# The first unit of scores of each batch's last, short block of tokens gets its earliest place one later

## The chip, the cores and the metric

The kernel runs on one core of a Trainium2 chip. The metric is the device time of one execution in microseconds (us); the median of several runs counts, and lower is better. One profiled execution gives the trace that the views below are read from.

## The reference

The kernel computes attention with the heads mixed twice, and a feed-forward network with a gate behind it:

```
# q, k, v: 8 batches x 12 heads x 448 tokens x 64
scores = (q @ k^T) / 8                        # per batch and head, 448 x 448
scores = einsum('bhij,hg->bgij', scores, w_pre)   # heads mixed, 12 x 12
attn   = softmax(scores) over j
attn   = einsum('bhij,hg->bgij', attn, w_post)    # heads mixed again
x      = (attn @ v), heads side by side       # 3584 tokens x 768
h      = x @ w_in                             # 768 -> 2048
out    = (h - tanh(h)) @ w_out                # 2048 -> 768
```

All of it is in float32; the feed-forward weights are split into parts by a conversion that runs during the attention.

## The kernel before

**Blocks, groups, places.** The 448 tokens of a batch are cut into four blocks of 120, 120, 120 and 88 tokens, so 32 blocks in all, numbered i = 0 to 31; the short one is i = 3, 7, 11, ..., 31. Ten tokens times 12 heads make a group of 120 rows (12 groups in a block, 9 in a short one), 360 groups in all. Two groups make a pair. The attention is a loop over 180 *places* (line 1262): place p takes pair p through the mixing of the heads and the softmax, and between these steps stand the other jobs that a list, `todo[p]`, gives to this place. On TensorE a place is, in this order:

- `premix(p)` (L920): four instructions (eight rows in the trace) that mix the heads of the pair's scores into two `ps_p` banks. The start of these rows is where a place begins in this text.
- the jobs of `todo[p]`
- `mix(p - 1)` (L957): the second mixing and the transposing of the pair before, which needs the factors `wr`.

VectorE then takes the maxima of place p (`mx`, L929) and ScalarE the exponentials (`e`, L931). The next place makes of their sums the reciprocals (`zs`, VectorE, L938 and L939) and of these the factors `wr` (GpSimd, L940), which `mix` waits for.

**The jobs.** All of them use the four banks `ps_m`/`ps_q` in turn.

- `prep_q(i, 0)`, `prep_q(i, 1)` (L842): transposes the queries of block i; ScalarE (`qh`, L855) and VectorE (`ql`, L857) take them out.
- `prep_k(b, hp)` (L816): the same for two heads of keys; `kk`, L827 on ScalarE and L828 on VectorE.
- `scores(i, hp)` (L876): six products for one pair of heads of block i into two banks. ScalarE and VectorE copy one bank each (L881) into the tile `s` of the block. A unit of scores is two of these jobs, three units make a block.
- `values(i, 0)`, `values(i, 1)` (L1000): the products with v, half a block each; VectorE copies the result to `x` (L1018).
- `load_q`, `load_k`, `load_v`: DMAs from the inputs.

**The tile `s` and the gathers.** `s` holds one block's scores for all heads, and there are two such tiles (`bufs=2`, L741), so block i writes where block i - 2 stood. A DMA on SyncE's queue, `gather(t)` (L909, `t<-s`), fetches group t's rows out of `s` into one of eight tiles `t`, three places ahead of its `premix`: place p issues the gathers 2p + 6 and 2p + 7. The copies of `scores(i, 0)` therefore have to wait until the last gather of block i - 2 has landed.

**Queues.** SyncE issues nearly all DMAs of this stage, in program order: the gathers of a place first, then up to six entries of a queue (loads, and the results that leave), and entries of a second queue with the traffic of the conversion of the feed-forward weights (`cr` in, `wi`/`ss`/`wo`/`ts` out, L767). The conversion (`narrow_quad`, L72) advances one phase in every place that is not in the set `short`, with work on VectorE (L81, L82, L90, L91, L94), ScalarE (L86, L99) and GpSimd (L84 to L129).

**The order.** The planner (L1154 to L1240) sets `todo`. Each unit of scores has an earliest and a latest place; for unit x of block i + 1 these are `e` and `hi`, where `f0`, `f1` are the first groups of blocks i and i + 1:

```
lo = max(0, (f0 - 1) // 2 - 2)
hi = f1 // 2 - 4
e = lo + 2 * x if lo + 4 <= hi else lo + (hi - lo) * x // 2
```

`lo` is the place behind the one that issues the last gather of block i - 1, whose tile `s` block i + 1 takes over. Values have such bounds too. The planner goes through the places in order and gives each one unit, the most urgent that may go, alternating between scores and values; afterwards a unit beside an empty place is split into two single `scores`. `prep_q` of a block is put at the place ahead of its first scores, `load_q` of the next block at the place behind that, and `prep_k` at the first place from a due one that is light enough and far enough behind the last use of its buffer. Within these rules every engine runs its instructions in the order written.

Of the kernel before, what the change touches and what calls it, by code (L numbers as in the profile page):

```python
# [148 lines left out]
def kernel_body(  # L149
# [524 lines left out]
    def pair_step(s, q, late, units, between):  # L674

        def product(i, ph, start):
            n = 7 * (s * NQ + q) + i
            more_wa(n + 6)
            name = WA[i][1]
            xs = [(ff.xs[name + "h"][:, c], ff.xs[name + "l"][:, c]) for c in range(HK)]  # L680
            products(ph, ff.wa.pop(n), xs, start, True)

        def rest(i):
            between(i)
            res.units(units[i])

        X, Y = hbank(), hbank()
        product(0, X, True)
        h01 = work("h01")
        nc.scalar.copy(h01[:, 1], X)  # L690
        if late:
            late.v0()
        rest(0)

        product(1, Y, True)
        nc.vector.tensor_add(h01[:, 1], Y, h01[:, 1])
        if late:
            late.v1()
        rest(1)

        product(2, X, False)
        if late:
            late.v2()
        h23 = work("h23")
        nc.scalar.mul(h23[:, 0], X, -1.0)
        if late:
            late.v3()
        rest(2)

        product(3, Y, True)  # L710
        if late:
            late.v4()
        nc.scalar.mul(h01[:, 0], Y, -1.0)
        rest(3)

        product(4, X, False)
        nc.vector.tensor_sub(h01[:, 0], h01[:, 0], X)  # L717
        if late:
            late.v5()
        g1 = Gate(h01, False)  # L720
        g1.a1()
        rest(4)

        product(5, Y, False)
        nc.vector.tensor_sub(h23[:, 0], h23[:, 0], Y)
        g1.a2()
        g1.d1()
        rest(5)

        product(6, X, False)  # L730
        nc.scalar.copy(h23[:, 1], X)
        g1.d2()
        g1.a3()
        rest(6)
        return Late(s, q, g1, Gate(h23))

    with ExitStack() as st:
# [344 lines left out]
        for w in range(2):  # L1082
            for at in AT[w]:
                x = repeat[:, w, at : at + HP].rearrange("p (i h) -> p i h", i=GH)
# [7 lines left out]
        for w in range(2):  # L1092
            for a in range(2):
                if w == 0:
                    x = both[:, w, a].rearrange("p (i g) -> p i g", i=GH)
                    of, step = ps_w[:, w, :].unsqueeze(1).to_broadcast([P, GH, H]), [[H, GH], [0, H]]
                else:
                    x = both[:, w, a].rearrange("p (g i) -> p g i", i=GH)
# [55 lines left out]
        halved = []  # L1154
        for i in range(len(blocks)):

            f0, f1, f2 = first[i : i + 3]
            if i + 1 < len(blocks):
                lo = max(0, (f0 - 1) // 2 - 2)
                hi = f1 // 2 - 4  # L1160
                for x in range(0 if i else 1, 3):
                    e = lo + 2 * x if lo + 4 <= hi else lo + (hi - lo) * x // 2
                    halved.append((e if i else x - 1, hi, "s", i + 1, x))
            for x in range(2):
                halved.append(((f1 - 1) // 2 + 2, f2 // 2 + 1 if f2 < NG else NPL + 7, "v", i, x))
        at_s, at_v, p, kind = {}, {}, 0, None
        window = {i: (lo, hi) for lo, hi, k, i, _ in sorted(halved, reverse=True) if k == "s"}
        while halved:
            ready = sorted((x for x in halved if x[0] <= p), key=lambda x: (x[1], x[3:]))
            if ready:  # L1170
                x = ready[0]
# [3 lines left out]
                if x[2] == kind and other and x[1] > p + 1:  # L1175
                    x = other[0]
                halved.remove(x)
                _, _, kind, i, n = x
# [11 lines left out]
        def held(p):  # L1190
            return [a for f, *a in todo[p] if f is scores]

        for p in range(1, NPL):
            if any(f in (scores, values) for f, *a in todo[p]):
                continue
            for of, n in ((p - 1, 1), (p + 1, 0)):
                if len(held(of)) == 2 and window[held(of)[n][0]][0] <= p <= window[held(of)[n][0]][1]:
                    i, hp = held(of)[n]
# [133 lines left out]
    late, left = None, 4 * NQ  # L1332
    for s in range(NS):
        more = s + 1 < NS
        for p in range(NQ):
# [16 lines left out]
            late = pair_step(s, p, late, share, between)  # L1352
# [16 lines left out]
        late = None  # L1369
# [33 lines left out]
```

## Time and profile before

| | |
|---|---|
| median of 3 runs | 1688.39 us (1685.31 to 1690.2) |
| profiled execution | 1691.88 us, of it 1690.2 us span |
| TensorE busy (PE) | 1654.1 us, 98% of the span |
| VectorE (DVE), ScalarE (ACT), GpSimd (POOL) busy | 1235.9, 1090.9, 613.9 us |
| the 180 places | 25.9 to 834.7 us of the span |

PE is TensorE, DVE is VectorE, ACT is ScalarE, POOL is GpSimd and SP is SyncE, which only issues DMAs. A line such as L957 is a line of the kernel; `ps_o<-wr,e` reads "writes ps_o, reads wr and e". In the view of waits, `A <- B: total, times, longest` says how long A's engine stood idle until B ended; in the timeline this stands in brackets behind a row. In the table by stretches, a row gives the stretch, its length, each engine's busy time, TensorE's granted clock (1.00 is full speed), the mean busy share of the DMA engines and GB/s.

### The profile page before, as it was taken

Reading aid. Unit: us, or ns where it says so; the run is one execution under the profiler, and the core shown is the slowest. Engines: PE = TensorE matmul, PEld = TensorE weight load, DVE = VectorE, ACT = ScalarE, POOL = GpSimd, SP = SyncE. Lnnn points to the kernel's source line nnn. Section 1 sums busy time; section 2 is a strip of 40 time slices with the busy share of each in tenths; the row PEclk is TensorE's granted clock in tenths of the full one; section 3 lists DMA queues with packets and bytes.
Section 4 is the critical chain, followed back from the end, with each engine's and each line's share of the span. In section 5 each row is a group of like instructions: output and inputs, shape, how many; then the busy total and the mean of one; then the engine's idle time right before and its main releaser. Section 6 shows DMA issues by size and latency. Waiting matters only on the chain.

```text
span 1690.2 us, 40990 instructions
## 1 busy us (share of the span) xinstructions
PE 1654.1 (98%) x16068; PEld 1380.8 (82%) x16068; DVE 1235.9 (73%) x1939; ACT 1090.9 (65%) x1896; POOL 613.9 (36%) x824
## 2 busy tenths in 40 slices
PE   8999999999999999999999999999999999999999
PEld 6777777777777777777788888888888888889999
DVE  5777786877867777776497999868778868778422
ACT  4777776677767677776576776556667356666331
POOL 2577666767666677664100111201111101012100
PEclk9999999999999999999999999999999999999999
DMA  9878788798978979875778899989999989988993
GB/s 191 232 249 239 248 245 253 236 269 256 260 229 260 257 246 261 263 238 201 229 248 321 286 324 319 346 288 343 330 324 358 358 272 338 325 321 321 412 413 134
DMA packets 322672, 475.08 MB, mean 281 GB/s; under 512 B 105648, under 2 KB 255664, under 8 KB 322480
## 3 DMA queue, kind: packets, MB, share of 16 engines
q1 hardware_dynamic: 305660, 414.34, 76.7%
q0 software_dynamic: 16512, 57.68, 8.6%
q8 instruction: 128, 2.10, 0.5%
q14 instruction: 64, 0.52, 0.1%
q10 hardware_dynamic: 308, 0.43, 0.1%
HBM read 274.73 MB, written 120.59 MB: 234 GB/s over the span
## 4 chain that ended last, share of the span: by engine, by line
PE 84%; DVE 6%; DMA 4%; ACT 3%; issue 2%; POOL 1%; SPq 0%; DVEq 0%; ACTq 0%; POOLq 0%
PE ps_o L957 14%; PE ps_m L1000 8%; PE ps_p L920 8%; PE ps_h L289 7%; PE ps_h L292 7%; PE ps_h L290 7%; PE y L532 6%; PE ps_q L876 6%; PE y L530 6%; PE y L531 6%; PE ps_m L842 1%; DMA w<-wo 1%; DMA t<-s 1%; PE ps_m L816 1%; DVE mx L929 1%
## 5 line engine op out<-in xcount | busy, mean ns | idle before, releaser
L957 PEld LDWEIGHTS ps_o<-wr,e 60*112 60x112 f32 (+1 forms) x5760 | 304.0, 175 | 32.7 <-POOL wr L940 17.2
L957 PE MATMUL ps_o<-wr,e 60*112 60x60 f32 (+1 forms) x5760 | 313.0, 258 | 7.0 <-POOL wr L940 5.7
L931 ACT ACTIVATE e<-ps_p,mx 128x448 f32<-128x448 f32 x360 | 225.4, 632 | 110.9 <-DVE mx L929 55.8
L929 DVE TENSOR_REDUCE mx<-ps_p 128x1 f32<-128x448 f32 x360 | 206.6, 616 | 78.6 <-PE ps_p L920 78.1
L967 ACT COPY at<-ps_o 112x960 f32<-112x960 f32 x156 | 153.9, 987 | 104.1 <-PE ps_o L957 103.7
L920 PE MATMUL ps_p<-t,wpre 60*64 60x448 f32 (+1 forms) x1440 | 179.1, 565 | 1.6 <-DMA t<-s 1.6
L940 POOL TENSOR_TENSOR wr<-wpost,zs 128x120 f32<-128x120 f32 x180 | 69.9, 388 | 265.6 <-DVE zs L939 204.8
L1000 PEld LDWEIGHTS ps_m<-at,vr 112*64 112x64 f32 x3072 | 151.2, 139 | 18.5 <-issue 12.9
L1000 PE MATMUL ps_m<-at,vr 112*64 112x120 f32 (+1 forms) x3072 | 164.8, 265 | 0.0
L530 PE MATMUL y<-w,gh 128*128 128x384 f32 x440 | 148.4, 337 | 4.1 <-DMA w<-wo 3.0
L531 PE MATMUL y<-w,gh 128*128 128x384 f32 x440 | 147.6, 336 | 0.0
L532 PE MATMUL y<-w,gl 128*128 128x384 f32 x416 | 140.4, 337 | 2.5 <-DVE gl L448 2.5
L881 DVE COPY s<-ps_q 120x448 f32<-120x448 f32 (+1 forms) x192 | 112.3, 615 | 24.6 <-DMA t<-s 12.5
L876 PEld LDWEIGHTS ps_q<-kk,qh 64*120 64x120 f32 (+1 forms) x768 | 58.6, 173 | 85.2 <-issue 44.6
L876 PE MATMUL ps_q<-kk,qh 64*120 64x448 f32 (+1 forms) x768 | 121.6, 393 | 1.2 <-DVE kk L828 0.5
L881 ACT COPY s<-ps_q 120x448 f32<-120x448 f32 (+1 forms) x192 | 94.8, 535 | 19.9 <-DMA t<-s 9.6
L305 ACT ACTIVATE u<-h 128x1024 f32<-128x1024 f32 x56 | 59.6, 1064 | 72.0 <-DVE h L717 68.1
L645 POOL DMA_DIRECT2D gs<-ga x24 | 17.5, 730 | 242.5 <-DVE ga L328 242.5
L530 PEld LDWEIGHTS y<-w,gh 128*128 128x128 f32 x440 | 82.6, 188 | 9.0 <-issue 4.7
L531 PEld LDWEIGHTS y<-w,gh 128*128 128x128 f32 x440 | 82.6, 188 | 3.3
L442 ACT CAST gh<-gl 128x1024 fp32r<-128x1024 f32 x60 | 62.5, 1041 | 28.7 <-DMA gl<-gs 18.0
L532 PEld LDWEIGHTS y<-w,gl 128*128 128x128 f32 x416 | 78.0, 188 | 3.4 <-DVE gl L448 3.4
(372 smaller groups left out, 3955.6 us busy)
## 6 DMA issues: line engine op xcount, KB each, us to landing
t<-s SPq DMA_DIRECT2D x342, 210.0 KB
wa<-ss SPq DMA_DIRECT2D x96, 384.0 KB
gl<-gs SPq DMA_DIRECT2D x62, 512.0 KB
w<-wo SPq DMA_DIRECT2D x41, 768.0 KB
wa<-wi SPq DMA_DIRECT2D x72, 384.0 KB
w<-ts SPq DMA_DIRECT2D x36, 768.0 KB
gs<-gs POOLq DMA_DIRECT2D x24, 768.0 KB, 8.5
cr<-in_moe_w_in_dram SPq DMA_DIRECT2D x48, 256.0 KB
```

The lines of the kernel that those rows point to most:

```text
L289: nc.tensor.matmul(ph, w[:, c, 0], xh, start=start and c == 0, stop=False, skip_group_check=True)
L530: nc.tensor.matmul(y, gh[:, tok], wh, start=first, stop=False, skip_group_check=True)
L531: nc.tensor.matmul(y, gh[:, tok], wl, start=False, stop=False, skip_group_check=True)
L532: nc.tensor.matmul(y, gl[:, tok], wh, start=False, stop=last, skip_group_check=True)
L876: nc.tensor.matmul(ps[:n, :S], qx[a, hp, :], kx[a, hp % 2], start=(x == 0), stop=(x == 2))
L881: eng(sts[i][:n, 2 * hp + j, :], ps[:n, :S])
L920: nc.tensor.matmul(pss[r][halves[j], :], wpre[k, :], ts[j][k, :], start=True, stop=True)
L929: nc.vector.tensor_reduce(out=mx, in_=ps, axis=AX.X, op=ALU.max, negate=True)
L931: nc.scalar.activation(e, ps, AF.Exp, bias=mx, scale=1.0, accum_out=zs[:, 0, r : r + 1])
L957: nc.tensor.matmul(ps[:CP, j, c * GP : (c + 1) * GP].rearrange("p (h i) -> p h i", i=GI)[:, :, r * GH : (r + 1) * GH], e[k, c * CP : (c + ...
L967: nc.scalar.copy(ats[i0][:, :, :, at : at + 2 * GI].rearrange("p c h (j i) -> p j (c h) i", j=2), ps[:CP, :, : NC * GP].rearrange("p j (x ...
L1000: nc.tensor.matmul(pv[j * D : (j + 1) * D, r, :n], vt[:, j, c, :], ats[i][:, c, 2 * hp + j, :n], start=(c == 0), stop=(c == NC - 1),)
```

## The change

The earliest place of unit 0 of the short block's scores is raised by one (`i % 4 == 2` means that block i + 1 is the short one). Nothing else is edited:

```
                 for x in range(0 if i else 1, 3):
                     e = lo + 2 * x if lo + 4 <= hi else lo + (hi - lo) * x // 2
-                    halved.append((e if i else x - 1, hi, "s", i + 1, x))
+                    late = 1 if i % 4 == 2 and x == 0 else 0
+                    halved.append((e + late if i else x - 1, hi, "s", i + 1, x))
```

The planner answers to it in each of the 8 batches, at four places in a row. For batch 2 (counted from 0; block 11 is its short one) these are places 53 to 56; the other batches' begin at places 8, 31, 76, 98, 121, 143 and 166:

| place | before | after |
|---|---|---|
| 53 | prep_q(11, 0 and 1), values(8, 0) | values(8, 0) |
| 54 | scores(11, 0), scores(11, 1), load_q(12) | prep_q(11, 0 and 1), values(8, 1) |
| 55 | prep_k(3, 2 and 3), values(8, 1) | scores(11, 0), scores(11, 1), load_q(12) |
| 56 | scores(11, 2) | prep_k(3, 2 and 3), scores(11, 2) |
| 57 | scores(11, 3) | the same |

The last batch has no prep_k and no load_q there. The set `short` stays the same.

TensorE in batch 2, before, from the rows behind `premix(53)` on (`ident,qr` is prep_q, `at,vr` values, `kk,qh` and `kk,ql` scores, `ident,kr` prep_k):

```order
L842 MATMUL ps_m<-ident,qr 128x88 x6
L1000 MATMUL ps_m<-at,vr 64x120 x24
L957 MATMUL ps_o<-wr,e 112x12x5 x16
L920 MATMUL ps_p<-t,wpre 64x448 x4
L876 MATMUL ps_q<-kk,qh 88x448 x4
L876 MATMUL ps_q<-kk,ql 88x448 x2
L876 MATMUL ps_q<-kk,qh 88x448 x4
L876 MATMUL ps_q<-kk,ql 88x448 x2
L957 MATMUL ps_o<-wr,e 112x12x5 x16
L920 MATMUL ps_p<-t,wpre 64x448 x4
L816 MATMUL ps_m<-ident,kr 128x112 x8
L1000 MATMUL ps_m<-at,vr 64x120 x24
```

The same stretch with the change, from the rows behind `premix(53)` on:

```order
L1000 MATMUL ps_m<-at,vr 64x120 x24
L957 MATMUL ps_o<-wr,e 112x12x5 x16
L920 MATMUL ps_p<-t,wpre 64x448 x4
L842 MATMUL ps_m<-ident,qr 128x88 x6
L1000 MATMUL ps_m<-at,vr 64x120 x24
L957 MATMUL ps_o<-wr,e 112x12x5 x16
L920 MATMUL ps_p<-t,wpre 64x448 x4
L876 MATMUL ps_q<-kk,qh 88x448 x4
L876 MATMUL ps_q<-kk,ql 88x448 x2
L876 MATMUL ps_q<-kk,qh 88x448 x4
L876 MATMUL ps_q<-kk,ql 88x448 x2
L957 MATMUL ps_o<-wr,e 112x12x5 x16
```

The first scores now stand behind both halves of the values, one `premix` and one `mix` later, and prep_k comes at the place behind them, ahead of the next single `scores` (not shown).

SyncE's queue in the same batch, where `t<-s` are the gathers, `cr` and `ss` the conversion's traffic and `qr` is load_q(12) (a piece of the difference):

```order
 L909 DMA t<-s 120x1x448 x4
-L767 DMA qr<-in_q_dram 120x12x64
 L767 DMA ss_81<-ct 512x1x256
 L767 DMA cr<-in_moe_w_in_dram 128x2x256 x2
 L909 DMA t<-s 120x1x448 x2
+L767 DMA qr<-in_q_dram 120x12x64
```

The gathers keep their order; load_q(12) goes behind three conversion DMAs and two more gathers.

## Prediction

> **What bounds the kernel now.** First the page's head, then the table by stretches for the 180 places of the attention.
>
> ```profile
> span 1690.2 us, 40990 instructions
> PE 1654.1 (98%) x16068; PEld 1380.8 (82%) x16068; DVE 1235.9 (73%) x1939; ACT 1090.9 (65%) x1896; POOL 613.9 (36%) x824
> ...
> 26.00:834.67 808.67, 793.82 (x11629) 613.27 (x11629) 596.75 (x1326) 581.66 (x1309) 509.36 (x639) 0.99 0.83 245
> ```
>
> TensorE is busy 98% of the span, in the attention 793.8 of 808.7 us. It is the bound, and the change takes no matmul away. What can be had is idle time of TensorE (14.9 us here) and time at a lower clock, so I next read the view of waits over this stage for what TensorE and the copies of the scores wait for.
>
> ```profile
> DVE s L881 <- DMA t<-s: 12.5, 3, 6.0
> ...
> PE ps_m L816 <- DVE s L881: 7.9, 4, 4.1
> ...
> PE ps_o L957 <- POOL wr L940: 5.7, 7, 1.3
> ```
>
> Four times the transposes of prep_k (L816) wait for VectorE's copies of scores, 7.9 us in all, and three times such a copy is seen waiting for a gather. To find the four, I cut the stage into places by the eight L920 rows that open each. The table by stretches has first the seven places that hold prep_k and values(., 1) of the first block of a batch (10, 33, 55, 78, 100, 123, 145), then three places with one scores job (79, 101, 102).
>
> ```profile
> 66.67:72.82 6.15, 6.15 (x98) 5.08 (x96) 4.74 (x11) 3.62 (x9) 4.46 (x4) 1.00 0.83 221
> 167.63:176.68 9.05, 7.84 (x98) 6.56 (x97) 6.00 (x14) 4.61 (x10) 4.41 (x7) 0.81 0.95 270
> 268.82:281.63 12.81, 8.71 (x98) 7.44 (x96) 5.09 (x11) 4.43 (x10) 3.38 (x7) 0.73 0.93 274
> 377.00:383.16 6.16, 6.16 (x99) 5.09 (x97) 4.72 (x10) 3.30 (x8) 4.03 (x4) 1.00 0.83 278
> 475.59:482.99 7.40, 6.22 (x98) 5.09 (x97) 4.38 (x10) 4.62 (x10) 3.48 (x6) 1.00 0.93 289
> 580.35:589.56 9.21, 7.83 (x99) 6.56 (x97) 5.09 (x11) 4.43 (x10) 3.46 (x6) 0.81 0.91 251
> 681.86:688.01 6.15, 6.15 (x98) 5.08 (x97) 4.66 (x11) 4.05 (x9) 3.99 (x4) 1.00 0.88 298
> ...
> 383.16:386.37 3.21, 3.21 (x48) 2.32 (x47) 1.92 (x5) 2.94 (x7) 0.39 (x1) 1.00 0.91 225
> ...
> 482.99:487.63 4.64, 3.56 (x49) 2.30 (x47) 4.12 (x12) 2.73 (x6) 1.22 (x2) 0.97 0.87 252
> 487.63:492.29 4.66, 4.66 (x49) 2.92 (x47) 2.11 (x5) 2.85 (x6) 3.07 (x3) 0.66 0.42 159
> ```
>
> The same work takes 6.15 us in batches 0, 3 and 6 and 9.05, 12.81, 7.40 and 9.21 us in batches 1, 2, 4 and 5: 2.90 + 6.66 + 1.25 + 3.06 = 13.87 us too much. In batch 4 the two places behind follow with 4.64 and 4.66 instead of 3.21: 2.88 us. Together 16.75 us. The clock column says why this is twice the idle time of the waits: behind the wait TensorE is granted 0.73 to 0.81.
>
> Now the cause, in batch 2: the timelines of TensorE, VectorE and SyncE.
>
> ```profile
> 268.82 0.98 PE L920 MATMUL ps_p<-t,wpre 60*64 60x448 f32 x8
> 273.90 1.76 PE L816 MATMUL ps_m<-ident,kr 112*128 112x112 f32 x8 [4.10 <-DVE s L881]
> 275.59 4.40 PE L1000 MATMUL ps_m<-at,vr 112*64 112x120 f32 x48
> ...
> 266.04 1.16 DVE L929 TENSOR_REDUCE mx<-ps_p 128x1 f32<-128x448 f32 x2 [0.45 <-PE ps_p L920]
> 273.22 1.15 DVE L881 COPY s<-ps_q 88x448 f32<-88x448 f32 x2 [6.03 <-DMA t<-s]
> ...
> 261.31 3.50 SPq L767 DMA_DIRECT2D ss<-ct  x1
> 264.90 2.06 SPq L767 DMA_DIRECT2D cr<-in_moe_w_in_dram  x2
> 267.05 1.69 SPq L909 DMA_DIRECT2D t<-s  x2
> ```
>
> The two gathers issued from 267.05 are 112 and 113, the last of block 9, whose tile `s` block 11 takes over. SyncE comes to them late, behind the conversion's traffic. They land just ahead of 273.22, where the copy starts; VectorE was free at 267.20 (266.04 + 1.16). So the copies are 6.0 us late, L816 finds no free bank, and TensorE idles 4.10 us. In the other three batches the copies are late by half of that:
>
> ```profile
> 169.15 1.15 DVE L881 COPY s<-ps_q 88x448 f32<-88x448 f32 x2 [3.14 <-DMA t<-s]
> ...
> 477.07 1.15 DVE L881 COPY s<-ps_q 88x448 f32<-88x448 f32 x2 [3.10 <-PE ps_p L920]
> ...
> 582.03 1.15 DVE L881 COPY s<-ps_q 88x448 f32<-88x448 f32 x2 [3.30 <-DMA t<-s]
> ```
>
> In 477.07 the view names TensorE, which had long been done; I read it as the same gather.
>
> **The change part by part.** It adds and removes no instruction. In each batch four places are dealt anew; a place costs TensorE what its matmuls cost, and rows of before show each new kind or its nearest neighbour.
>
> ```profile
> 220.52:225.76 5.24, 5.24 (x90) 4.31 (x88) 3.95 (x8) 2.44 (x6) 4.16 (x5) 1.00 0.92 265
> 259.15:264.99 5.84, 5.84 (x96) 4.82 (x94) 4.53 (x11) 3.56 (x9) 5.09 (x7) 1.00 0.95 243
> 264.99:268.82 3.83, 3.83 (x54) 2.79 (x53) 1.73 (x5) 2.32 (x5) 3.08 (x3) 1.00 1.02 274
> 247.54:251.70 4.16, 4.16 (x57) 3.18 (x55) 3.37 (x7) 2.92 (x7) 1.41 (x2) 1.00 0.85 253
> 251.70:255.29 3.59, 3.50 (x48) 2.32 (x47) 3.13 (x8) 3.24 (x8) 2.16 (x3) 1.00 0.92 241
> ...
> 458.27:461.50 3.23, 3.23 (x48) 2.38 (x46) 2.99 (x8) 2.59 (x7) 2.22 (x3) 1.00 1.06 277
> ...
> 664.70:667.94 3.24, 3.24 (x48) 2.40 (x46) 3.00 (x8) 2.58 (x7) 2.21 (x3) 1.00 0.92 240
> ...
> 48.37:53.15 4.78, 3.50 (x48) 2.32 (x46) 4.61 (x12) 3.41 (x8) 2.08 (x3) 1.00 0.88 216
> ```
>
> Row 1 is values alone (place 44), row 2 prep_q with values (53), row 3 a unit of scores (54), row 4 prep_k with one scores job (50). Before, the four places cost 5.84 + 3.83 + 6.15 + 3.21 = 19.03 us without waits; after, 5.24 + 5.84 + 3.83 + 4.16 = 19.07 us. That is +0.04 us a batch, 0.3 us in eight.
>
> *The copies against the gather.* The scores begin 5.24 + 5.84 = 11.08 us behind the start of the first of the four places instead of 5.84, so 5.24 us later, while the gathers keep their place in SyncE's queue. Of the 6.03 us of lateness in batch 2 about 0.8 us is left, of the 3.1 to 3.3 us in the others nothing. What TensorE bears without a stall follows from batch 2: 6.03 us of lateness became 4.10 us of idle, so about 1.9 us is covered by the `mix` and `premix` that stand ahead of L816. 0.8 us lies inside. So the 16.75 us go, the two places behind batch 4's stall included, since their wait for `wr` came out of the copies' delay. Bounds: 0 gained, if the gathers move with the scores, and 16.75.
>
> *prep_q and values(., 1)* change places with prep_q hidden as before, one place ahead of its scores; values need nothing but what values(., 0) already had a place earlier. I take 0; if the 5.84 did not hold, the nearest rows for what the same place can vary by are 5 and 6, 0.36 us apart, in eight batches 2.9 us either way.
>
> *prep_k beside one scores job.* VectorE gets two `kk` subtractions into this place, ahead of the `zs` that the next place's `wr` and `mix` wait for; TensorE would wait at that `mix`. The trace has this pair of places four times. The place behind took 3.59, 3.23 and 3.24 us (rows 5 to 7), and 4.78 us once (row 8, with one more phase of conversion beside it). From row 6, between nothing and 4.78 - 3.23 = 1.55 us a batch. I take the mean of the three that are like the new places (no conversion phase in the place behind), 0.12 us, in seven batches with prep_k 0.8 us.
>
> *load_q of the next block* is issued one place later, behind two more gathers and in batch 2 behind three conversion DMAs:
>
> ```profile
> 274.13 0.76 SPq L767 DMA_DIRECT2D qr<-in_q_dram  x1
> ...
> 279.08 1.65 SPq L909 DMA_DIRECT2D t<-s  x2
> ```
>
> It would go out at about 280.8 instead of 274.1. With the 6.2 us from 267.05 to 273.22 as a time to land that is 287.0. Its reader, place 59, comes at 259.15 + 19.07 + 3.21 + 3.83 = 285.3, plus 0.9 of `premix`. If SyncE does not come earlier by itself, that is 0.8 us late, in this batch alone. But SyncE's issues here wait on the conversion, which the stalled VectorE had held up; I take 0, with 0.8 us kept for the range. ScalarE's and VectorE's copies move with their matmuls; GpSimd gets no instruction moved.
>
> The sum: 16.75 - 0.3 - 0.8 = 15.6 us. The profiled execution took 1691.88 us and would take 1676.3. The median, 1688.39, lies 3.5 us below it, and the same difference gives 1672.8.
>
> **The clock behind a short wait.** A wait that is left over can cost more than itself. In batch 5 TensorE idled 1.38 us (9.21 less 7.83 busy), and a stretch at half clock followed:
>
> ```profile
> 582.95:586.36 3.41, 3.41 (x30) 3.13 (x30) 1.84 (x6) 3.41 (x9) 2.32 (x3) 0.50 0.76 235
> ```
>
> Half of 3.41 us is 1.7 us; with the 1.38 us of idle that is the 3.06 us lost there. Row 8 is the other bound: 1.28 us of idle (4.78 less 3.50) at a clock of 1.00 all through. So a leftover wait of 1 us costs 1.0 to 2.7 us; I take 2.7, the dearer row, because the stalls in question are like batch 5's. The Trainium skill (TensorE: Matmul & The Clock Gate, Part 1: The HAM clock gate) says that the clock is halved after at least one idle window of about 3.4 us. By that rule only batch 2's wait would have lost clock, and two leftover waits of 1 us would make 1674.8 us of the forecast where the row above makes 1678.2. The trace speaks against it: 1.38 us were enough in batch 5. It agrees on the length of the slow stretch, 3.41 us.
>
> **The rivals.**
>
> 1. *A part comes back.* The copies in batch 2 and the `kk` work leave waits of about 1 us in two to four places, at 2.7 us each: 5.4 to 10.8 us of the 15.6 come back, which gives 1678.2 to 1683.6. For it: rows 5 and 8; against it: rows 6 and 7.
> 2. *The transfers are the bound.* In batch 2 the DMA share is 1.02 in the place ahead of the stall; if transfers set the pace, TensorE waits at a `premix` or for `qr` instead, and the time stays 1688.4. Against it: the share over the stage is 0.83, and batches 0, 3 and 6 run these places without a wait at 0.83 to 0.88.
> 3. *Slower: `mix` waits for `wr` behind the new prep_k place in every batch.* At row 8's 1.55 us and a half clock of 1.7 us, seven batches lose 22.8 us: 1688.4 - 16.45 + 22.8 = 1694.7. It decides from 2.4 us a batch on. Against it: three of four such places lost 0.35 us at most.
>
> **How the numbers follow.** The stalls go with little given back: 62%, 1668 to 1677. Rival 1: 17%. Rival 2: 13%. Rival 3: 8%. A measurement of this kernel tells some 0.3% (5.1 us) from no change: faster by more 79%, within 13%, slower 8%. The range has at its low end all 16.75 us from the fastest run shown (1685.3), 1668, less 1 us; at its high end rival 1 whole and a little of rival 2: 1667 to 1685.
>
> **What would show it.** Right: places 33, 55, 100 and 123, now scores alone, at 3.8 us, the places behind at 4.2, no wait of L816 for `s`, and no clock below 1.00 between 100 and 800 us. Wrong: L881 still waits over 2 us for `t<-s`; or L957 waits for `wr` at places 12, 35, 57; or L842 of place 59 waits for `qr`.

## The result, and the profile after

The changed kernel takes 1680.99 us, the median of 16 runs (1679.35 to 1685.35), beside 1689.76 us (16 runs, 1685.31 to 1696.22) for the kernel before on the same chip: 8.8 us less. The ratio is 0.9949, its 95% interval 0.9938 to 0.9961. The forecast was 1672.8 us, so the direction is right and the gain is little more than half of the 15.6 us. The head of the profile after:

```profile
PE 1654.7 (98%) x16068; PEld 1379.2 (82%) x16068; DVE 1243.4 (74%) x1939; ACT 1091.3 (65%) x1896; POOL 612.8 (36%) x824
```

The profiled execution took 1685.35 us, the longest of the 16. Places 0 to 7, which the change leaves alone, took 36.9 us in it and 31.1 us in the profile of before; this is taken up below. The table by stretches has places 33, 35, 55 to 59, 100 and 123 of the profile after, and then the whole attention:

```profile
175.13:178.96 3.83, 3.83 (x55) 2.78 (x53) 3.71 (x10) 3.61 (x8) 2.61 (x4) 1.00 0.92 295
...
183.08:186.63 3.55, 3.47 (x48) 2.25 (x46) 3.08 (x8) 3.18 (x8) 2.15 (x3) 1.00 0.93 201
...
274.55:278.37 3.82, 3.82 (x55) 2.79 (x53) 2.65 (x5) 3.54 (x8) 2.06 (x3) 1.00 0.83 282
278.37:282.61 4.24, 4.24 (x57) 3.02 (x55) 3.42 (x7) 3.37 (x9) 2.10 (x4) 1.00 0.91 309
282.61:286.46 3.85, 3.54 (x49) 2.36 (x47) 3.70 (x8) 3.48 (x9) 2.16 (x3) 1.00 1.05 250
286.46:291.02 4.56, 4.09 (x55) 2.70 (x53) 4.53 (x9) 2.73 (x8) 3.78 (x5) 1.00 0.83 250
291.02:297.02 6.00, 6.00 (x96) 4.92 (x95) 3.74 (x9) 3.86 (x10) 4.25 (x7) 1.00 0.88 307
475.95:479.78 3.83, 3.83 (x54) 2.79 (x52) 3.71 (x10) 3.60 (x8) 2.61 (x4) 1.00 0.92 292
...
576.94:580.77 3.83, 3.83 (x55) 2.79 (x53) 2.78 (x5) 3.54 (x8) 2.15 (x2) 1.00 0.82 297
...
26.16:828.82 802.66, 793.00 (x11629) 610.27 (x11629) 603.46 (x1326) 582.13 (x1309) 509.97 (x639) 0.99 0.82 247
```

The four stalls are gone: places 33, 55, 100 and 123 take 3.82 or 3.83 us at full clock, where 9.05, 12.81, 7.40 and 9.21 us stood. But places 35 and 57, which took 3.21 us before, now take 3.55 and 3.85, and places 58 and 126 (the latter not shown) take 4.56 and 4.55 instead of 3.88 and 3.86. The attention as a whole is 6.0 us shorter (802.66 against 808.67). The view of waits over the attention says what TensorE and the copies wait for now:

```profile
PE ps_o L957 <- POOL wr L940: 7.6, 11, 1.8
...
DVE s L881 <- PE ps_q L876: 6.2, 13, 1.5
```

There is no row any more of L881 waiting for `t<-s` or of L816 waiting for `s`. In their place `mix` waits for `wr` 11 times, 7.6 us in all, where the view of before had 7 times and 5.7 us. Five of the 11 are new, 1.9 us together, at places 57, 58, 125, 126 and 148. The timelines around places 57 and 58 show the first two. VectorE first:

```profile
276.80 1.15 DVE L881 COPY s<-ps_q 88x448 f32<-88x448 f32 x2
...
282.72 1.16 DVE L828 TENSOR_TENSOR kk<-ps_m,kk 128x448 fp32r<-128x448 f32 x2 [0.83 <-ACT kk L827]
283.79 0.16 DVE L938 TENSOR_SCALAR zs<-zs 128x2 f32<-128x2 f32 x1
...
285.65 1.34 DVE L81 TENSOR_SCALAR cm<-cr 128x512 f32<-128x512 f32 x1
286.91 1.53 DVE L82 TENSOR_SCALAR cr<-cr 128x512 int32<-128x512 int32 x1
288.37 0.15 DVE L938 TENSOR_SCALAR zs<-zs 128x2 f32<-128x2 f32 x1
```

Twice `zs` comes behind other work of VectorE. GpSimd, which makes `wr` of it, in the same stretch:

```profile
284.30 0.39 POOL L940 TENSOR_TENSOR wr<-wpost,zs 128x120 f32<-128x120 f32 x1 [3.46 <-DVE zs L939]
...
285.21 1.50 POOL L96 TENSOR_TENSOR cm<-cr,co 128x512 f32<-128x512 f32 x1
286.79 1.37 POOL L97 TENSOR_TENSOR cm<-cm,cr 128x512 f32<-128x512 f32 x1
288.86 0.39 POOL L940 TENSOR_TENSOR wr<-wpost,zs 128x120 f32<-128x120 f32 x1 [0.70 <-PE ps_q L876]
```

And TensorE, which waits for `wr`:

```profile
284.74 1.78 PE L957 MATMUL ps_o<-wr,e 60*112 60x60 f32 x32 [0.31 <-POOL wr L940]
...
289.30 0.90 PE L957 MATMUL ps_o<-wr,e 60*112 60x60 f32 x14 [0.47 <-POOL wr L940]
```

In place 57, VectorE waits 0.83 us for ScalarE's part of `kk` and takes the two subtractions of the place before at 282.72, then `zs` at 283.79, `wr` follows at 284.30 and `mix` at 284.74, 0.31 us late. In place 58, the conversion's next phase (L81, L82, 2.8 us of VectorE) stands ahead of `zs`, and `mix` is 0.47 us late. That phase stood ahead of `zs` in before too, where the two steps took 0.8 us (last section). The first row is the copy of the moved scores: it no longer waits for anything in the view. The view has 0.31 us of wait in place 57, which grew by 0.64. `mix` begins 2.13 us behind the start of the place (284.74 less 282.61), where before it began 1.59 us behind it (286.52 less 284.93, not shown): 0.54 us later. Part of this does not show as idle time, because TensorE's rows overlap where one job follows on the other: before, the last scores row reached to 286.68. `mix` itself takes 1.78 us instead of 1.69. So the busy time of the place grew as well (3.54 us instead of 3.21).

### The profile page after: what moved, and what is told of

Same layout as the page of the kernel before. It is cut to its first block, busy times and chain, and to the rows that moved or that the text cites. A ratio compares the mean times of both kernels' runs of the same rounds, so it can differ in the third digit from the quotient of the medians.

```text
span 1683.6 us, 40980 instructions
## 1 busy us (share of the span) xinstructions
PE 1654.7 (98%) x16068; PEld 1379.2 (82%) x16068; DVE 1243.4 (74%) x1939; ACT 1091.3 (65%) x1896; POOL 612.8 (36%) x824
## 4 chain that ended last, share of the span: by engine, by line
PE 83%; DVE 6%; DMA 4%; ACT 4%; issue 2%; POOL 1%; SPq 0%; DVEq 0%; POOLq 0%; ACTq 0%
PE ps_o L957 14%; PE ps_m L1000 8%; PE ps_p L920 8%; PE ps_h L289 7%; PE ps_h L290 7%; PE ps_h L292 7%; PE y L532 6%; PE y L530 6%; PE y L531 6%; PE ps_q L876 6%; DMA w<-wo 1%; PE ps_m L842 1%; DMA t<-s 1%; ACT e L931 1%; PE y L502 1%
## 5 line engine op out<-in xcount | busy, mean ns | idle before, releaser
L957 PEld LDWEIGHTS ps_o<-wr,e 60*112 60x112 f32 (+1 forms) x5760 | 304.7, 175 | 36.5 <-POOL wr L940 20.8
L957 PE MATMUL ps_o<-wr,e 60*112 60x60 f32 (+1 forms) x5760 | 314.7, 259 | 8.9 <-POOL wr L940 7.6
L1000 PEld LDWEIGHTS ps_m<-at,vr 112*64 112x64 f32 x3072 | 147.6, 137 | 22.0 <-issue 14.1
L1000 PE MATMUL ps_m<-at,vr 112*64 112x120 f32 (+1 forms) x3072 | 161.1, 261 | 0.0
L881 DVE COPY s<-ps_q 120x448 f32<-120x448 f32 (+1 forms) x192 | 112.4, 615 | 8.9 <-PE ps_q L876 8.5
L881 ACT COPY s<-ps_q 120x448 f32<-120x448 f32 (+1 forms) x192 | 95.0, 536 | 7.0 <-PE ps_q L876 6.7
```

Of the source, the lines that this page charges most:

```text
L881: eng(sts[i][:n, 2 * hp + j, :], ps[:n, :S])
L957: nc.tensor.matmul(ps[:CP, j, c * GP : (c + 1) * GP].rearrange("p (h i) -> p h i", i=GI)[:, :, r * GH : (r + 1) * GH], e[k, c * CP : (c + ...
L1000: nc.tensor.matmul(pv[j * D : (j + 1) * D, r, :n], vt[:, j, c, :], ats[i][:, c, 2 * hp + j, :n], start=(c == 0), stop=(c == NC - 1),)
```

## The experiments

The theory (A): the late gathers cost the four stalls; the move takes them away in the four batches that had them; in the others it brings nothing. The first rival (B): the new dealing of jobs is cheaper by itself, with a stall or without.

**The move in the four stalled batches alone.**

```
-late = 1 if i % 4 == 2 and x == 0 else 0
+late = 1 if i in (6, 10, 18, 22) and x == 0 else 0
```

> The later place is given to the scores of batches 1, 2, 4 and 5 alone, the four in which the copies into s waited for a gather. Theory A (what is gained is those waits, 16.75 us of them in the trace of before, less about 5 us that come back at mix): all of the gain of the full change, 8 to 12 us faster than before, and batch 6 as before (its place 148 at 3.9 us, not 4.4). Theory B (the new dealing of values and prep_k is itself cheaper, in every batch): half of the gain, 4 to 5 us.

1681.46 us (6 runs, 1679.01 to 1685.22), ratio to before 0.9943, interval 0.9925 to 0.9962: 7.7 us less than before on the same chip (1689.11 us), a little under the 8 to 12 expected, and within the noise all of the gain. Its table by stretches has place 33 as it is after, and place 148, in batch 6 that was not moved, as it was before:

```profile
169.94:173.75 3.81, 3.81 (x54) 2.79 (x52) 3.68 (x10) 3.58 (x8) 2.60 (x4) 1.00 0.93 305
...
682.41:686.31 3.90, 3.90 (x55) 2.71 (x53) 3.83 (x9) 3.41 (x9) 3.12 (x5) 1.00 0.83 277
```

**The move in the other four batches alone.**

```
-late = 1 if i % 4 == 2 and x == 0 else 0
+late = 1 if i in (2, 14, 26, 30) and x == 0 else 0
```

> The later place is given to the scores of batches 0, 3, 6 and 7 alone, which had no such wait. Theory A: nothing is gained, 0 to 1 us slower than before, and the stalls of batches 1, 2, 4 and 5 stand in the profile as before (places 33, 55, 100, 123 at 9, 13, 7 and 9 us). Theory B: 4 to 5 us faster.

1690.53 us (12 runs, 1687.18 to 1694.62), ratio 1.0003, interval 0.9987 to 1.0019. Nothing is gained, and B falls. One part of the expectation was missed: the stalls of places 33, 55, 100 and 123, untouched here, were not as long as in the profile of before:

```profile
169.27:175.69 6.42, 6.22 (x98) 5.09 (x96) 4.38 (x10) 4.66 (x10) 3.58 (x7) 1.00 0.95 285
269.13:281.37 12.24, 8.52 (x98) 7.25 (x97) 5.09 (x11) 4.43 (x10) 3.37 (x7) 0.72 0.94 283
...
475.26:481.42 6.16, 6.16 (x98) 5.09 (x96) 4.63 (x11) 4.54 (x10) 3.84 (x6) 1.00 0.89 278
577.26:583.96 6.70, 6.23 (x99) 5.09 (x97) 4.35 (x10) 4.43 (x10) 3.46 (x6) 1.00 0.87 249
```

Only batch 2 stalls as before; in place 100 there is no stall to see. So the price of the stalls moves from execution to execution, or with what the other batches do; the repeated profiles below bear on this. The profiled execution, 1687.65 us, is the second fastest of the 12.

**The order before, with the last gathers sent first.** The scores stay, but at the seven places that issue the last gathers of the block whose `s` is taken over, SyncE holds the conversion's traffic back for one place.

```
-def issue(most):
-    for x in (queue, slow):
+def issue(most, of):
+    for x in of:
...
-issue(6)
+issue(6, (queue,) if p in (7, 30, 52, 75, 97, 120, 142) else (queue, slow))
```

> The kernel before, with the conversion's DMAs held back in one place of each of seven batches (7, 30, 52, 75, 97, 120, 142), so that SyncE issues the last gathers of the block whose s is taken over ahead of them; no other engine's order changes. Theory A (the copies are late because SyncE comes to these gathers late): the gather of batch 2 goes out 5 to 6 us earlier, batch 4's about 5, batch 5's 2.4, batch 1's 0.6; the stalls at places 55, 100 and 123 go, that at 33 keeps 2 to 3 us; 10 to 14 us faster than before, without moving the scores. Theory D (the transfers are the bound, whatever their order): the gathers land at the same time or TensorE waits elsewhere, within 4 us of before.

1683.39 us (12 runs, 1678.10 to 1691.21), ratio 0.9958, interval 0.9938 to 0.9978. The cause is shown: nothing but SyncE's order was touched, and 5.7 us of 1689.11 go. Places 33, 34 and 55 in the table by stretches, and VectorE's copy that waited 6.03 us in batch 2:

```profile
167.96:174.43 6.47, 6.23 (x99) 5.09 (x97) 3.99 (x9) 4.12 (x10) 3.07 (x6) 1.00 0.89 295
174.43:179.56 5.13, 3.46 (x48) 2.24 (x47) 4.52 (x12) 3.06 (x8) 1.74 (x3) 1.00 0.99 241
...
268.45:275.00 6.55, 6.23 (x99) 5.09 (x97) 4.36 (x10) 4.44 (x10) 3.40 (x7) 1.00 0.91 294
...
269.08 1.15 DVE L881 COPY s<-ps_q 88x448 f32<-88x448 f32 x2 [2.25 <-PE ps_o L957]
```

The copy waits 2.25 us, and place 55 falls from 12.81 to 6.55 us, place 123 (not shown) from 9.21 to 6.16. The 10 to 14 us expected were not reached. Less than expected was won in batch 1, where place 33 keeps 0.3 us and place 34, at 5.13 instead of 3.21 us, waits for `wr` (1.67 us of idle); that is 2.2 us, and the rest stays open.

**The change without the conversion's phase beside the new prep_k.** It tests what came back: the phase is left out of the seven places that now hold prep_k and one scores job, and all later phases shift.

```
+short |= {11, 34, 56, 79, 101, 124, 146}
 block0 = Block0()
```

> The changed kernel, with no phase of the conversion in the seven places that now hold prep_k and one scores job (11, 34, 56, 79, 101, 124, 146); the conversion runs one place behind for each. Theory A (mix waits at places 57, 58, 125 and 126 because VectorE has the conversion's three operations and two kk subtractions there ahead of zs): L957's waits for wr at 57 and 125 go and those places take 3.2 to 3.3 us, 2 to 4 us faster than the changed kernel. Theory C (the waits come from the banks or from transfers, not from VectorE's load): the waits stay and the time is that of the changed kernel within 1 us.

1679.68 us (7 runs, 1677.95 to 1688.20), ratio 0.9943, interval 0.9922 to 0.9965; it cannot be told from the change itself, so the 2 to 4 us expected beyond it were missed. Places 57 and 58, and places 166 to 179 together:

```profile
275.66:278.88 3.22, 3.22 (x48) 2.25 (x46) 3.02 (x8) 2.59 (x7) 2.16 (x3) 1.00 0.90 177
278.88:283.23 4.35, 4.09 (x55) 2.71 (x53) 4.32 (x9) 2.88 (x8) 3.56 (x5) 1.00 0.63 228
...
757.74:822.18 64.44, 61.81 (x925) 47.60 (x923) 38.92 (x87) 42.27 (x94) 32.40 (x46) 0.97 0.69 236
```

Place 57 is back at 3.22 us, so its wait needs both, the conversion's phase and `kk`, ahead of `zs`; places 35, 102 and 125 (not shown) are back at 3.22 us too. But place 58 keeps 4.35, and the conversion, ending seven places later, reaches the last places: 64.44 us instead of 61.63 in the profile after (of the 2.8 us, 1.5 are half clock in the last place, which other profiles have too). The saving is shifted, not won.

**Both kernels again, unedited.** Two more profiles of before and two of after, to size the 16.75 us.

> The kernel before, unedited, for a second profile. It sizes the 16.75 us that the prediction took for the four stalls from one execution. In that one batches 1, 2, 4 and 5 lost 2.90, 6.66, 4.13 and 3.06 us, and two of the four stalls were followed by 3.41 to 6.83 us at half clock. Theory A: the idle time of the stalls is steady (about 7.9 us of waits of L816), and the half clock behind them comes and goes, so that places 33, 55, 100 to 102 and 123 together lose anywhere from 9 to 17 us; expected here about 11 us, with stretches at half clock in other places than in the first profile. Theory B: the stalls cost the same in each execution, 16 to 17 us, with half clock behind places 33, 55 and 123 again; then some 4 us that the change should have brought went elsewhere. Time 1685 to 1692 us.

> The kernel before, a third profile, for the spread of the same sum. Theory A: places 33, 55, 100 to 102 and 123 lose 9 to 17 us over 6.15 us for the first four and 3.21 us for the places 101 and 102, not the same as in the second profile. Theory B: 16 to 17 us as in the first. The time and the mean granted clock should go together: 0.001 of the clock is 1.7 us.

> The changed kernel, unedited, for a second profile. In the first, places 0 to 7, whose code the change does not touch, took 36.9 us where they took 31.1 in the profile of before. Theory A: that is a chance of the one execution; here 31 to 33 us, and 1680 to 1682 us in all. Theory B: it belongs to the change; here again about 37 us. Either way what came back behind the moved jobs is steady, as it comes from the order and not from the clock: places 35, 57, 102 and 125 at 3.5 to 3.9 us instead of 3.2, places 58 and 126 at 4.5 instead of 3.85, place 148 at 4.4 instead of 3.9, about 4 to 5 us in all.

> The changed kernel, unedited, timed beside the other and beside before on one chip. 1681 us, 0.995 of before; slow windows of 3.41 us begin at whole multiples of 3.41 us from each other, as in the profiles so far; of the waits of TensorE of 1.0 to 1.4 us in places 4 to 166 those that lie within one such window are followed by half clock about two times in three, those that straddle two windows are not.

The profiled executions took 1689.86 and 1699.08 us (before), 1681.03 and 1685.21 us (after). Six more runs of after had a median of 1681.04 us, against 1688.62 us of before (12 runs) on the same chip, ratio 0.9957, interval 0.9944 to 0.9969. The table by stretches, for places 31 to 75 (batches 1 and 2) and 98 to 142 (batches 4 and 5). First the profile of before that the prediction read:

```profile
157.96:367.33 209.37, 203.59 (x2954) 158.22 (x2953) 156.85 (x345) 148.28 (x335) 141.26 (x179) 0.98 0.85 247
465.92:672.19 206.27, 202.35 (x2954) 156.48 (x2952) 155.62 (x344) 148.33 (x335) 138.06 (x166) 0.98 0.86 251
```

The second profile of before:

```profile
159.04:369.62 210.58, 203.78 (x2955) 158.48 (x2953) 156.80 (x345) 148.30 (x335) 141.07 (x179) 0.98 0.84 246
468.17:670.62 202.45, 199.55 (x2954) 154.49 (x2952) 155.25 (x344) 148.42 (x335) 137.54 (x166) 1.00 0.87 255
```

The first profile of after:

```profile
164.05:366.33 202.28, 200.20 (x2954) 154.34 (x2952) 159.90 (x345) 148.61 (x335) 141.57 (x179) 1.00 0.87 258
464.87:665.75 200.88, 199.79 (x2954) 154.41 (x2952) 159.32 (x344) 148.33 (x335) 138.28 (x166) 1.00 0.87 256
```

And the second:

```profile
157.72:359.54 201.82, 200.28 (x2954) 154.34 (x2953) 160.39 (x344) 148.58 (x335) 141.93 (x179) 1.00 0.87 257
458.11:658.99 200.88, 199.78 (x2955) 154.39 (x2953) 159.26 (x344) 148.35 (x335) 138.27 (x166) 1.00 0.87 258
```

The two stretches summed, those of the third profiles with them, split into TensorE's idle time (length less busy) and busy time:

| profile | length | idle | busy | the stalls* |
|---|---|---|---|---|
| before, first | 415.64 | 9.70 | 405.94 | 16.75 |
| before, second | 413.03 | 9.70 | 403.33 | 13.21 |
| before, third | 415.75 | 10.51 | 405.24 | 15.72 |
| after, first | 403.16 | 3.17 | 399.99 | none |
| after, second | 402.70 | 2.64 | 400.06 | none |
| after, third | 402.29 | 2.41 | 399.88 | none |

*Places 33, 55, 100, 123, 101 and 102 over 6.15 us and 3.21 us, the sum that the prediction made. It leaves out what place 124 lost in the second profile (0.75 us) and place 34 in the third (1.34 us).

Both theories about the size were partly right. The idle time is steady, as A said, and it is half clock that comes and goes; but 13.2 to 16.8 us is a narrower band than A's. The four batches gain 12.1 us in the mean, of it 7.2 us of idle and 4.9 us of busy time, which is half clock less what the matmuls of after are spread out. This is more than the medians show: the three profiled executions of before have a mean of 1693.6 us, above all its medians (1688.39 to 1691.77 us). The profile of the move in the other four batches, where these four batches are as in before, has 7.65 us of idle and 7.95 us of stalls, outside the spread of the three; so the price of a stall moves with what the other batches do as well. Places 0 to 7 of the kernel after took 30.9 us in the second profile and 33.8 in the third, so their 36.9 us in the first are not in every execution. Whether they have to do with the change stays open: `mix` of place 4 waits 1.5 to 2.2 us for `wr` in three of the 12 profiles, all three of kernels with the move in batch 0 (six profiles), though none of their instructions ahead of place 8 differ. What came back is the same in all three, within 0.03 us: places 35, 57, 102 and 125 at 3.55, 3.85, 3.55 and 3.84 us.

**Two attempts at a better version.** The move in the four stalled batches, or in all eight, and the phase left out at four places.

```
-late = 1 if i % 4 == 2 and x == 0 else 0
+late = 1 if i in (6, 10, 18, 22) and x == 0 else 0
...
+short |= {34, 56, 101, 124}
 block0 = Block0()
```

> The move in the four batches that stalled, and the conversion's phase left out of places 34, 56, 101 and 124 alone, the new places with prep_k. Theory A (the wait for wr there comes of the conversion beside kk): places 35, 57, 102 and 125 at 3.2 us, 36, 58, 103 and 126 up by at most 0.5 us, places 166 to 180 at 63.1 us, up by 1.5, since the conversion ends four places later; the time 1679 us, 2 us less than the change as it is, in the range of 1677 to 1681. Rival: what the skipped phases save, the shifted phases take back in other places (as places 36, 103 and 165 did where all seven were left out), and the time is 1681, that of the four batches alone.

1683.68 us (12 runs, 1680.61 to 1689.96), ratio 0.9955, interval 0.9938 to 0.9971, on a chip where before took 1691.77 us: the rival, as by the ratio it cannot be told from the move in the four batches alone (0.9943). The profile shows where the saving went. Places 78 and 145 of the table by stretches, in batches 3 and 6 that were not moved:

```profile
368.45:376.52 8.07, 6.23 (x99) 5.09 (x97) 4.33 (x10) 4.66 (x10) 3.55 (x7) 1.00 0.92 265
...
669.01:676.29 7.28, 6.22 (x98) 5.08 (x96) 4.38 (x10) 4.64 (x10) 3.47 (x6) 1.00 0.94 297
```

They stall now (before they took 6.15 or 6.16 us in every profile but one, where place 145 took 6.80): the conversion, shifted, falls ahead of their last gathers, and in place 78 the copy waits 3.76 us for `t<-s`. Which batch stalls is a matter of where the conversion stands. With the move in all eight batches, as the change has it, and the same four phases left out:

> The change in all eight batches, as it is, with the conversion's phase left out of places 34, 56, 101 and 124 alone. Theory A (moving the scores by one place makes a batch proof against where the conversion's traffic falls; the batches that were left as before are at its mercy, as places 78 and 145 with 8.06 and 7.29 us showed where the same four phases were left out): places 78 and 145, now scores alone, at 3.83 us, no wait of L816 for s, places 35, 57, 102 and 125 at 3.22 us; batches 121:143 and 143:166 within 1 us of the changed kernel's 99.9 and 101 to 103; the time 1679 us, 1677 to 1681. Rival: the shifted phases take back what they save in any order; the time is that of the changed kernel on this chip, or above.

1680.03 us (6 runs, 1676.64 to 1683.44), ratio 0.9953, interval 0.9939 to 0.9967, beside 1681.04 us for the change itself on the same chip. Place 78:

```profile
369.13:372.96 3.83, 3.83 (x54) 2.79 (x52) 2.77 (x5) 3.54 (x8) 2.06 (x3) 1.00 0.82 296
```

Place 145 takes 3.83 us too. In none of the three places of the conversion that were run with the move in all batches (the change, and the phase left out of seven places or of four) did a moved batch stall; that is what the move is good for in the batches that did not need it. In the four batches this version takes 399.4 us, 3.4 less than after in the mean, yet its time cannot be told from that of the change. Part of the 3.4 us is paid in batch 3, where places 76 to 97 take 99.9 us instead of 98.5 or 98.6: with the phases shifted, places 79 to 81 take 4.32, 3.84 and 4.56 us instead of 4.13, 3.22 and 4.17, the last two with `mix` 0.31 and 0.47 us late, as in places 57 and 58 of the change.

## Why the prediction was right in direction and too large

- **The bound and the cause: right.** TensorE's idle time and clock were what could be had, and the late gathers were the cause: the experiment that touched SyncE's order alone shortened place 55 by 6.3 us.
- **Where the gain is: right.** All of it lies in batches 1, 2, 4 and 5.
- **The places' nominal costs: right.** 5.24 and 5.84 us for places 53 and 54, 3.82 for 55, and 4.13 where nothing came back, as the rows of before had them.
- **The copies in batch 2: a little better than said.** 0.8 us of lateness was left over for them; the copy at 276.80 waited for nothing.
- **load_q: right.** Place 59 took 6.00 us, as before, with no wait for `qr`.
- **The 16.75 us: too large, by 1 to 3.5.** The term came from one execution, 3.5 us above the median, and the sum was carried over to the median as if the 3.5 us lay elsewhere. The other two profiles of before have 13.21 and 15.72 us in the same six places. The idle time of the first two was the same (9.70 us in both); stretches at half clock make their difference. The 13.21 us belong to an execution of 1689.86 us, close to the medians; but the 15.72 us belong to one of 1699.08 us, so the time of an execution does not tell what its stalls cost, and the term is known no more closely than this.
- **The 0.8 us for prep_k beside one scores job: too small, by 3.4.** In the second profile of after, places 35, 57, 102 and 125 are 0.33, 0.64, 0.33 and 0.62 us over before's 3.21 or 3.22; the places behind them, 58 and 126, which the prediction did not price, 0.68 and 0.70; places 56 and 124 0.20 each over 4.13; place 148 0.53 over 3.90. That is 4.2 us: 1.9 in the places right behind prep_k, which the term was for, and 2.3 in places without a term. The step that failed took the mean of three neighbours without a conversion phase in the place behind. What counts is a phase beside prep_k itself: with it left out, the four places right behind were back at 3.22 us. It has to be one that keeps VectorE ahead of `zs`: places 12, 80 and 147 lost nothing in the change, but 80 and 147 took 3.84 and 3.55 us when the phases were shifted. In place 58 the phase stood before as well, at 3.88 us. New there is that `wr` of place 57 comes 1.69 us behind the place's start (284.30 less 282.61) instead of 0.36 us, so GpSimd's next steps, L96 and L97, come later and meet VectorE's L81 and L82 in another order; this is read from the rows, no run tests it alone.

13.2 - 4.2 = 9.0 us, and 1689.9 - 9.0 = 1680.9, against 1680.99 measured. That it comes out so closely is in part luck: with the mean of the three sums, 15.2 us, it would be 11.0 us. The result lies inside the range of 1667 to 1685 us, but above the 1668 to 1677 us that had 62%. It is in the range of the first rival, which had 17%: a part comes back, and by its mechanism. But the rival's price was wrong: not two to four waits of 1 us with half clock behind them, but nine places that lost 0.2 to 0.7 us each, at full clock.

Of the signs named in advance, those for right were seen (3.8 us, 4.1 to 4.3 us behind, no wait of L816, no clock below 1.00 between 100 and 800 us in the first profile; the second has one such stretch, behind place 164), and one of those for wrong as well: L957 waits for `wr` at place 57.

The two profiles at the medians also show what noise there is beyond the change. In the four batches the second profile of after is 10.3 us shorter than the second of before; in the whole span 8.9. Half clock fell into places 165 and 179 of the one and place 7 of the other, about 1.5 us each time.

## What to carry to other kernels

Size a stall from more than one execution before its half clock is counted: here the idle part was steady between executions of one kernel and the clock part was not. When work is moved out of a wait, price also the place where it lands and the one behind, with what else already stands there on the engine that feeds the bound. A move that frees a consumer from a late transfer may be worth making in all like places, not only in those that stall in today's profile, since which ones stall depends on where the other traffic falls. Here the time does not decide it: the move in four batches and in all eight gave the same gain (0.9943 and 0.9949 of before), and only the profiles with shifted phases tell them apart.

## What the runs showed of the hardware

**Half clock runs on a grid.** In each of the 12 profiles the stretches at half clock begin whole multiples of 3.413 us apart (in that of before after 42, 72, 135 and 163 of them from the first). One wait, `mix` of place 6 for `wr`, is 1.28 or 1.29 us long in ten of them. The table by stretches, cut on the grid; the profile of before first, then that of the move in the four stalled batches, then that of the move in the other four:

```profile
47.08:50.49 3.41, 3.07 (x42) 1.89 (x40) 3.07 (x7) 3.01 (x7) 0.00 (x0) 1.00 0.90 196
50.49:53.91 3.42, 2.47 (x40) 1.86 (x40) 3.38 (x8) 2.40 (x6) 2.83 (x3) 1.00 0.75 224
53.91:57.32 3.41, 3.41 (x52) 2.93 (x52) 3.04 (x9) 2.40 (x7) 2.16 (x4) 1.00 0.89 222
```

The wait in one window:

```profile
49.48:52.89 3.41, 2.13 (x38) 1.86 (x40) 3.37 (x8) 2.02 (x6) 2.45 (x3) 1.00 0.80 216
52.89:56.30 3.41, 3.41 (x20) 2.06 (x14) 2.85 (x6) 2.26 (x6) 2.38 (x3) 0.50 0.74 242
```

And in one window once more:

```profile
49.97:53.39 3.42, 2.14 (x22) 1.01 (x22) 3.24 (x9) 2.05 (x4) 0.78 (x2) 1.00 0.71 211
53.39:56.80 3.41, 3.41 (x48) 2.53 (x48) 3.38 (x8) 2.44 (x6) 2.62 (x4) 1.00 0.67 236
```

In the first the wait straddles two windows (0.34 and 0.95 us of idle), and the clock stays at 1.00. In the second it lies in one (1.28 us), and the next window runs at 0.50. In the third it lies in one as well, and nothing follows. Of 32 waits of TensorE of 1.0 to 1.4 us in places 4 to 164 of all profiles (one of them with 0.01 us in the window ahead is counted to its second), 13 straddled two windows, and none of these was followed by half clock; 19 lay in one, and 13 were. Why not the other six is open. Five waits of 1.19 us in place 179 straddled and were followed, but there the window ahead had 1.08 to 1.42 us of idle in all. What holds in the attention need not hold elsewhere: in the feed-forward part the profile of before has four waits of 1.43 to 2.34 us and no half clock until the last 2 us. The Trainium skill (TensorE: Matmul & The Clock Gate, Part 1: The HAM clock gate) says that the window is free-running and does not reset when a kernel starts; the grid agrees, and with it goes that the same wait costs 1.3 us in one execution and 2.8 in the next. Its rule that half clock comes after an idle window of about 3.4 us does not hold here: 1.0 to 1.4 us in one window were enough.

**The clock goes with the spread.** Over the 52 runs of before that have a clock on record (one more, of 4069.91 us at a clock of 1.00, is left out), time and mean granted clock correlate at -0.91 (1682.75 us at 0.998, 1696.2 us at 0.988). The mean clock is 0.9933 in these and 0.9961 in 23 runs of after. 0.0028 of 1690 us is 4.7 us, of 8.5 us between the mean times.

**A conversion step can take three times as long beside GpSimd.** L81 took 1.34 us at 285.65 and L82 1.53 us at 286.91, while GpSimd ran L96 until 286.71 and L97 until 288.16. In the profile of before, in the 36 cases where no step of GpSimd ran beside them, they took 0.40 to 0.43 us. But the neighbour alone does not make them slow. The same phase in before, VectorE and GpSimd:

```profile
287.58 0.41 DVE L81 TENSOR_SCALAR cm<-cr 128x512 f32<-128x512 f32 x1
287.92 0.43 DVE L82 TENSOR_SCALAR cr<-cr 128x512 int32<-128x512 int32 x1
288.25 1.26 DVE L938 TENSOR_SCALAR zs<-zs 128x2 f32<-128x2 f32 x1
...
287.58 1.91 POOL L97 TENSOR_TENSOR cm<-cm,cr 128x512 f32<-128x512 f32 x1
```

Here L97 started together with L81, and it was L97 that took longer, 1.91 us where the median of its 48 is 1.35, and behind it the short `zs`, 1.26 us instead of 0.16. The Trainium skill (SBUF — State Buffer, SBUF: two separate sides) says that VectorE and GpSimd share a pair of ports as an exclusive lock, held for the whole instruction; the two slow steps of after end 0.28 us behind GpSimd's, as that would have it. No run took the sharing away, so the cause is argued, not shown.
